# A state-space attention block and two MLPs on one core: GpSimd work in 256-column pieces, attention four levels a tile, the second MLP's weight decoding over three tiles

## The chip, the cores and the metric

The kernel runs on 1 core of one Trainium2 chip. The metric is the device time of a run in microseconds (us); three runs of the kernel before gave 609.05 to 609.72 us, with a median of 609.28 us.

## The reference

```python
def _attn_ref(x, a, B, C):                      # x (4, 8, 768, 32), B and C (4, 8, 768, 16)
    log_a = np.log(np.clip(a, 1e-06, 1.0))
    for c in range(S // 32):
        cum = np.cumsum(la, axis=-1)
        M = einsum('bhin,bhjn->bhij', Cc, Bc) * exp(cum_i - cum_j) * causal
        y[:, :, sl] = einsum('bhij,bhjd->bhid', M, xc) + einsum('bhin,bhnd->bhid', Cc, state) * exp(cum)
        state = exp(sum(la)) * state + sum_j Bc_j xc_j exp(cum_last - cum_j)

def _moe_ref(x, w_in, w_out):                   # x (3072, 256), w_in (256, 2048), w_out (2048, 256)
    h = np.maximum(x @ w_in, 0.0)
    return h * h @ w_out

def _moe2_ref(x, w_in, w_out):
    h = x @ w_in
    return (h * clip(h + 3.0, 0.0, 6.0) / 6.0) @ w_out

reference = _moe2_ref(_moe_ref(attention output as (3072, 256)))
```

## The kernel before

**Attention** runs in 12 levels of 64 positions of all four batches (NLEV). A level l is a handful of named jobs: `load` (six DMAs on SP's queue: C and B transposed, B and x by token, and last the decay factors `ef`), `scale` (GpSimd multiplies `ef` into the tile `bc`), `head` (ScalarE makes `cb` from `bc`), `tok` (GpSimd), `state` and `chunk` (TensorE bursts: the old state's part and the state's update; the part inside the level, and the next level's scores), `mask` and `adv` (VectorE), `high` and `low` (ScalarE and VectorE write the level's output as a high and a low fp32r part). Two levels make one tile of 512 tokens for the MLPs. The table PLAN says in which step of which tile each job is written.

**The first MLP** takes 6 tiles (t) of 512 tokens in 16 steps (f) of 128 hidden units; step number g = 16 t + f runs from 0 to 95. In a step (`step`, `gate`) TensorE makes h with six matmuls (`mm1`, L498), ScalarE takes the relu (L507), VectorE multiplies (L509), ScalarE makes the high part gh (L511), VectorE the low part gl (L513), and two steps later (LAG) TensorE adds h's part to y with six matmuls (`mm2`, L527). Each product is three fp32r matmuls: high by high, high by low, low by high. Levels 2 and 3 are done beside tile 0, levels 4 to 11 beside tiles 1 to 3, three levels a tile (five steps a level). After the last one the pools of the attention are closed (LASTATT) and wpool2 takes their room.

**The second MLP** takes pairs of tiles (3 pairs) in 8 quads, 24 quads g (`Quad`, `emit`). A quad is a Strassen step: seven products of sums of weights and sums of tokens (`product`, L620), ScalarE and VectorE for the gate, and 24 matmuls into y (`second`, L665). The token operands of a pair are made once: GpSimd makes the sums t1 to t4 (`oper_sum`, L565), ScalarE the high parts (`oper_high`, L576), VectorE the low parts (`oper_low`, L580).

**Weights** arrive as 64-bit floats and are decoded on the chip (`Weights`): a DMA of 512 KB a chunk j (L410), `early` on ScalarE (L421), `join` on VectorE in three operations (sign L425, bits L430, merge L435), then for the first MLP `split` (ScalarE L462, GpSimd L463), and for the second MLP `sums` (four GpSimd operations of 128 columns, L444), `high` (ScalarE, L478) and `lower` (GpSimd, 896 columns for an even chunk and 512 for an odd one, L483). The 16 chunks of the second MLP are decoded in steps 64 to 95, eight groups q of two chunks, four steps a group: join of the even chunk at step 64 + 4q, of the odd one two steps later.

The order of all this is the order in which the Python code writes it: each engine runs its instructions in that order and waits on semaphores. `at(g, point)` puts a job of the second MLP at a step (or, with 1000 added, at one of five points of a quad).

Of the kernel before, what the change touches and what calls it, by code (L numbers as in the profile page):

```python
# [964 lines left out]
```

## Time and profile before

| | us |
|---|---|
| median of three runs | 609.28 |
| the profiled execution, its own time | 613.11 |
| its span (first to last instruction) | 611.2 |
| TensorE busy (L498, L527, L620, L665 above all) | 569.9 |
| VectorE busy | 439.3 |
| ScalarE busy | 350.6 |
| GpSimd busy | 114.0 |
| mean granted TensorE clock, of full speed | 0.967 |

In the rows below PE is TensorE, PEld its weight loads, DVE VectorE, ACT ScalarE, POOL GpSimd and SP the queue that issues the DMAs. A row of the timeline gives the start in us, the duration in us, the engine, the line, the operation and its tiles with their shapes; in brackets stands how long the engine had been idle before it and what ended that. Matmul durations overlap; their starts give the pace.

### The profile page before, as it was taken

To read this page: it belongs to the slowest core of one execution; us is meant where nothing else is said; L and a number is where in the kernel's file an instruction comes from. 1 tells how busy PE (TensorE), PEld (TensorE's weight loads), DVE (VectorE), ACT (ScalarE), POOL (GpSimd) and SP (SyncE) were. 2 spreads that over 40 slices of the span, in tenths; PEclk is the share of its full clock that TensorE was granted. 3 is DMA by queue.
4 is the path that set the end of the run, shared out by engine and by line. 5 is a ranking of instruction groups with operands and counts; after the bars stand their busy time and mean duration, and the time that the engine had idled before them with its cause. 6 is when DMAs were issued, how large, how long until landed. Compare 5 with 4: busy or idle time off the path is not lost. (4 is left out here: it accounts for less than half of the span.)

```text
span 611.2 us, 11012 instructions
## 1 busy us (share of the span) xinstructions
PE 569.9 (93%) x4451; PEld 452.6 (74%) x4451; DVE 439.3 (72%) x672; ACT 350.6 (57%) x615; POOL 114.0 (19%) x117
## 2 busy tenths in 40 slices
PE   6587999999999999998987689999799999999996
PEld 3456787777778888876866468888588888788885
DVE  6598984556555545788788787677967778867674
ACT  4365755445445444664645556667666667766663
POOL 5252430011111000444355540000400000000000
PEclk9687999999999999999998889999989999999999
DMA  7771422221223000322231000000110000200002
GB/s 202 242 234 39 130 60 62 63 58 27 60 61 114 1 3 0 104 69 80 93 91 48 1 1 0 1 1 1 29 41 0 1 1 1 69 2 0 1 1 70
DMA packets 32802, 31.46 MB, mean 51 GB/s; under 512 B 14608, under 2 KB 27376, under 8 KB 32752
## 3 DMA queue, kind: packets, MB, share of 16 engines
q1 hardware_dynamic: 31408, 30.37, 17.1%
q8 instruction: 35, 0.57, 0.4%
q10 hardware_dynamic: 1344, 0.39, 0.3%
q14 instruction: 15, 0.12, 0.1%
HBM read 27.41 MB, written 3.35 MB: 50 GB/s over the span
## 5 line engine op out<-in xcount | busy, mean ns | idle before, releaser
L509 DVE TENSOR_TENSOR ga<-ga,ha 128x512 f32<-128x512 f32 x96 | 65.7, 685 | 54.6 <-ACT ga L507 54.1
L511 ACT ACTIVATE gha<-ga 128x512 fp32r<-128x512 f32 x96 | 60.8, 633 | 69.2 <-DVE ga L509 69.2
L513 DVE TENSOR_TENSOR gla<-ga,gha 128x512 fp32r<-128x512 f32 x96 | 69.8, 727 | 33.9 <-ACT gha L511 33.8
L527 PE MATMUL ya<-gla,ah 128*128 128x512 f32 x192 | 77.4, 403 | 14.1 <-DVE gla L513 14.1
L507 ACT ACTIVATE ga<-ha 128x512 f32<-128x512 f32 x96 | 56.7, 591 | 52.1 <-PE ha L498 52.1
L498 PE MATMUL ha<-act_h,ah 128*128 128x512 f32 x192 | 77.0, 401 | 5.9 <-DVE ga L509 5.1
L527 PE MATMUL ya<-gha,ah 128*128 128x512 f32 x192 | 78.4, 408 | 0.0
L665 PE MATMUL y<-glc,bh 128*128 128x512 f32 x192 | 75.8, 395 | 1.3 <-DVE glc L651 1.3
L498 PE MATMUL ha<-act_h,al 128*128 128x512 f32 x192 | 76.4, 398 | 0.0
L527 PE MATMUL ya<-gha,al 128*128 128x512 f32 x192 | 76.1, 396 | 0.0
L498 PE MATMUL ha<-act_l,ah 128*128 128x512 f32 x192 | 76.1, 396 | 0.0
L665 PE MATMUL y<-ghc,bh 128*128 128x512 f32 x192 | 75.6, 394 | 0.0
L665 PE MATMUL y<-ghc,bl 128*128 128x512 f32 x192 | 75.5, 393 | 0.0
L651 DVE TENSOR_TENSOR glc<-c,ghc 128x512 fp32r<-128x512 f32 x96 | 68.3, 715 | 6.7 <-ACT ghc L648 6.3
L634 ACT ACTIVATE rc<-c,three 128x512 f32<-128x512 f32 x72 | 51.9, 720 | 29.4 <-DVE c L629 28.9
L642 DVE SCALAR_TENSOR_TENSOR c<-rc,c 128x512 f32<-128x512 f32 x72 | 51.8, 720 | 23.3 <-ACT rc L634 23.3
L648 ACT ACTIVATE ghc<-c 128x512 fp32r<-128x512 f32 x96 | 58.2, 629 | 3.5 <-DVE c L642 3.4
L527 PEld LDWEIGHTS ya<-gla,ah 128*128 128x128 f32 x192 | 36.7, 191 | 26.5 <-DVE gla L513 18.9
L629 DVE TENSOR_TENSOR c<-Z,u 128x512 f32<-128x512 f32 x48 | 33.1, 690 | 27.6 <-PE Z L620 27.6
L498 PEld LDWEIGHTS ha<-act_h,ah 128*128 128x128 f32 x192 | 37.2, 194 | 14.6 <-DVE ga L509 5.6
L665 PEld LDWEIGHTS y<-glc,bh 128*128 128x128 f32 x192 | 36.5, 190 | 10.2 <-DVE glc L651 2.5
L625 ACT COPY u<-X 128x512 f32<-128x512 f32 x48 | 28.1, 585 | 27.6 <-PE X L620 27.6
(213 smaller groups left out, 998.1 us busy)
## 6 DMA issues: line engine op xcount, KB each, us to landing
rawa<-in_w1i SPq DMA_DIRECT2D x8, 512.0 KB
rawa<-in_w1o SPq DMA_DIRECT2D x8, 512.0 KB
rawb<-in_w2i SPq DMA_DIRECT2D x8, 512.0 KB
rawb<-in_w2o SPq DMA_DIRECT2D x8, 512.0 KB
xb<-in_x SPq DMA_DIRECT2D x24, 128.0 KB
out_yT<-xf SPq DMA_DIRECT2D x12, 256.0 KB
ef<-scr SPq DMA_DIRECT2D x10, 256.0 KB
bc<-in_cT SPq DMA_DIRECT2D x12, 128.0 KB
```

The lines of the kernel that those rows point to most:

```text
L498: nc.tensor.matmul(out=h, lhsT=wt[fb][:, k, fo * P:fo * P + P], rhs=xt[t][:, k, :], start=i == 0, stop=i == 5)
L507: nc.scalar.activation(out=g, in_=h, func=AF.Relu)
L509: nc.vector.tensor_tensor(out=g, in0=g, in1=h, op=ALU.mult)
L511: nc.scalar.activation(out=gh, in_=g, func=AF.Copy)
L513: nc.vector.tensor_tensor(out=gl, in0=g, in1=gh.bitcast(F32), op=ALU.subtract)
L527: nc.tensor.matmul(out=ys[m], lhsT=terms[i][0][fb][:, fo, m * P:m * P + P], rhs=terms[i][1], start=f == 0 and i == 0, stop=f == NF - 1 and ...
L629: nc.vector.tensor_tensor(out=self.sb[c], in0=self.ps[bank], in1=self.sb[n], op=ALU.add)
L634: nc.scalar.activation(out=self.sb["r" + c], in_=src, func=AF.Relu, bias=three)
L642: nc.vector.scalar_tensor_tensor(out=self.sb[c], in0=self.sb["r" + c], scalar=6.0, in1=src, op0=ALU.min, op1=ALU.mult)
L648: nc.scalar.activation(out=self.gh[c], in_=self.sb[c], func=AF.Copy)
L651: nc.vector.tensor_tensor(out=self.gl[c], in0=self.sb[c], in1=self.gh[c].bitcast(F32), op=ALU.subtract)
L665: nc.tensor.matmul(out=ys[t][m], lhsT=terms[i][0][:, 7 + 2 * (1 - f) + m], rhs=terms[i][1], start=first and i == 0, stop=last and i == 2, ...
```

## The change

Five things are edited. (1) GpSimd's operations of 512 and 896 columns (`scale`, `split`, `lower`, `oper_sum`) are written as pieces of 256 columns. (2) Levels 4 to 11 take four steps each, four levels a tile, so that the attention ends with tile 2 (LASTATT 3 to 2) and wpool2 opens in tile 3. (3) The 16 chunks of the second MLP's weights are decoded from step 48 on, eight groups that begin at steps 48, 54, 60, 66, 72, 79, 86 and 91 instead of every four steps from 64; `high` and `lower` come one step later after the joins. (4) The operands of pair 0 are made over steps 80 to 95 instead of 89 to 95, those of pairs 1 and 2 over the four quads before the pair instead of mostly in the last one. (5) To make room, buffers move: the first MLP's raw chunks 3 to 9 lie in other places and chunk 12's DMA is written in step 6 instead of 4, act_l of tiles 0 to 2 becomes one tile that holds group 4's weights later, and operands take turns in PLACES.

```diff
-LASTATT = 3
+LASTATT = 2
...
 for _l in range(4, 12):
-    _s = 16 * ((_l - 4) // 3 + 1) + 5 * ((_l - 4) % 3)
-    for _k, _v in ((0, (f"mask{_l}", f"tok{_l}")), (1, (f"scale{_l + 1}",)), (2, (f"state{_l}", f"head{_l + 1}")),
-                   (3, (f"chunk{_l}", f"adv{_l}", f"load{_l + 2}")), (4, (f"high{_l}",)), (5, (f"low{_l}",))):
...
+    for _k, _v in ((0, (f"mask{_l}", f"tok{_l}", f"scale{_l + 1}")), (1, (f"head{_l + 1}",)), (2, (f"state{_l}",)),
+                   (3, (f"chunk{_l}", f"high{_l}", f"adv{_l}", f"load{_l + 2}")), (4, (f"low{_l}",))):
+        _d = PLAN.setdefault((4 * _l + _k) // 16, {})
...
-QKEEP = 4
+QKEEP = 3
...
+PLACES = ("l3", "l4", "w6", "w8", "w9", "w10", "w11", "raw", "raw", "wt", "wt", "l5")
...
-        (eng or nc.gpsimd).tensor_tensor(out=flat, in0=lev[l].pop("ef"), in1=flat, op=ALU.mult)
+        n = 4 if eng else 2
+        for b in range(0, NB, n):
+            (eng or nc.gpsimd).tensor_tensor(out=flat[:, b:b + n], in0=ef[:, b:b + n], in1=flat[:, b:b + n], op=ALU.mult)
...
-            nc.gpsimd.tensor_tensor(out=lo, in0=wt, in1=hi.bitcast(F32), op=ALU.subtract)
+            for k in range(2):
+                nc.gpsimd.tensor_tensor(out=lo[:, k], in0=wt[:, k], in1=hi[:, k].bitcast(F32), op=ALU.subtract)
...
-            d = slice(s.start - 1, s.stop - 1)
-            nc.gpsimd.tensor_tensor(out=self.lo[j // 2][:, d], in0=self.wt[j // 2][:, s],
-                                    in1=self.hi[j // 2][:, d].bitcast(F32), op=ALU.subtract)
+            for i in range(s.start, s.stop, 2):
+                k = slice(i, min(i + 2, s.stop))
+                d = slice(k.start - 1, k.stop - 1)
+                nc.gpsimd.tensor_tensor(out=self.lo[j // 2][:, d], in0=self.wt[j // 2][:, k],
+                                        in1=self.hi[j // 2][:, d].bitcast(F32), op=ALU.subtract)
...
-        pool, tag = (ps_y, "y") if 16 * t + f >= 68 and f % 4 > 1 else (ps_h, "h")
+        pool, tag = (ps_y, "y") if 16 * t + f >= 52 and f % 4 > 1 else (ps_h, "h")
...
-        nc.gpsimd.tensor_tensor(out=f[n], in0=f[i0], in1=f[i1], op=ALU.subtract)
+        for k in range(2):
+            c = slice(TOK // 2 * k, TOK // 2 * (k + 1))
+            nc.gpsimd.tensor_tensor(out=f[n][:, c], in0=f[i0][:, c], in1=f[i1][:, c], op=ALU.subtract)
...
-        for j in {0: (6, 7), 1: (8,), 2: (9,), 3: (10, 11), 4: (12,), 7: (13,), 8: (14,), 10: (15,)}.get(f, ()):
+        for j in {0: (6, 7), 1: (8,), 2: (9,), 3: (10, 11), 6: (12,), 7: (13,), 8: (14,), 10: (15,)}.get(f, ()):
...
-    for q in range(NQ):
-        base = 64 + 4 * q
-        late = 2 * (q == QNEW)
+    for q, base in enumerate((48, 54, 60, 66, 72, 79, 86, 91)):
+        late = 2 * (q == QNEW + 1)
         for dg, p, f, j in ((-1, 0, "early", 0), (0, 0, "join", 0), (0, 0, "sums", 0), (1, 0, "early", 1), (2, 0, "join", 1),
-                            (2 + late, 1, "high", 0), (2 + late, 1, "lower", 0), (3 + late, 1, "high", 1),
-                            (3 + late, 1, "lower", 1)):
+                            (3 + late, 1, "high", 0), (3 + late, 1, "lower", 0), (4 + late, 1, "high", 1),
+                            (4 + late, 1, "lower", 1)):
...
-        for n, dg, p in (("t1", -2, 4), ("t2", -1, 0), ("t3", -1, 4), ("t4", 0, 0), ("b11", 0, 0)):
-            at(1000 + g + dg, p, lambda n=n: oper_sum(key, n))
-        for i, n in enumerate(OPS):
-            for d, f in ((0, oper_high), (1, oper_low)):
-                dg, p = divmod(i + d, 5)
-                at(1000 + g + dg, p, lambda f=f, n=n: f(key, n))
...
+    operands(0, ("b", 0), ((80, 0, "s", "b11"), (81, 0, "h", "b11"), (82, 0, "l", "b11"), (83, 0, "s", "t1"), (83, 0, "h", "b21"),
+                           (84, 0, "l", "b21"), (89, 0, "s", "t2"), (90, 0, "h", "t2"), (90, 0, "s", "t3"), (91, 0, "l", "t2"),
+                           (92, 0, "h", "t3"), (92, 0, "l", "t3"), (93, 0, "h", "t1"), (93, 0, "s", "t4"), (94, 0, "l", "t1"),
+                           (94, 0, "h", "t4"), (95, 0, "l", "t4"), (1000, 0, "h", "b22"), (1000, 1, "l", "b22")))
+    for p in range(1, NPAIR):
+        operands(1000 + NQ * p, ("b", p),
+                 ((-4, 0, "s", "t1"), (-4, 1, "s", "b11"), (-4, 1, "h", "b11"), (-4, 2, "l", "b11"), (-4, 3, "s", "t2"),
+                  (-4, 4, "h", "b21"), (-3, 0, "l", "b21"), (-3, 0, "s", "t3"), (-3, 2, "h", "t2"), (-3, 3, "l", "t2"),
+                  (-3, 3, "s", "t4"), (-2, 0, "h", "t3"), (-2, 1, "l", "t3"), (-2, 3, "h", "t1"), (-2, 4, "l", "t1"),
+                  (-1, 1, "h", "t4"), (-1, 2, "l", "t4"), (-1, 3, "h", "b22"), (-1, 4, "l", "b22")))
```

VectorE's order around one group of the second MLP's weights (`lowb` rows are a join; `ga` and `gla` are the two operations of every step). Before, group 3 in tile 4:

```order
L509 TENSOR_TENSOR ga_12_3402<-ga_12_3402,ha_12_3393 128x512
L425 TENSOR_SCALAR lowb_3412<-rawb_3311 128x512
L430 TENSOR_SCALAR lowb_3412<-rawb_3311 128x512
L435 SCALAR_TENSOR_TENSOR wtb_3390<-wtb_3390,lowb_3412 128x512
L513 TENSOR_TENSOR gla_12_3401<-ga_12_3402,gha_12_3400 128x512
L509 TENSOR_TENSOR ga_13_3432<-ga_13_3432,ha_13_3423 128x512
L513 TENSOR_TENSOR gla_13_3431<-ga_13_3432,gha_13_3430 128x512
L509 TENSOR_TENSOR ga_14_3453<-ga_14_3453,ha_14_3444 128x512
L425 TENSOR_SCALAR lowb_3467<-rawb_3366 128x512
L430 TENSOR_SCALAR lowb_3467<-rawb_3366 128x512
L435 SCALAR_TENSOR_TENSOR wtb_3390<-wtb_3390,lowb_3467 128x512
```

With the change, from the odd chunk of group 1 to the even one of group 2, in tile 3:

```order
L441 SCALAR_TENSOR_TENSOR wtb_2925<-wtb_2925,lowb_2998 128x512
L526 TENSOR_TENSOR gla_8_2987<-ga_8_2988,gha_8_2986 128x512
L522 TENSOR_TENSOR ga_9_3014<-ga_9_3014,ha_9_3005 128x512
L526 TENSOR_TENSOR gla_9_3013<-ga_9_3014,gha_9_3012 128x512
L522 TENSOR_TENSOR ga_10_3041<-ga_10_3041,ha_10_3032 128x512
L526 TENSOR_TENSOR gla_10_3040<-ga_10_3041,gha_10_3039 128x512
L522 TENSOR_TENSOR ga_11_3064<-ga_11_3064,ha_11_3055 128x512
L526 TENSOR_TENSOR gla_11_3063<-ga_11_3064,gha_11_3062 128x512
L522 TENSOR_TENSOR ga_12_3086<-ga_12_3086,ha_12_3077 128x512
L431 TENSOR_SCALAR lowb_3096<-rawb_2951 128x512
```

The joins were two steps apart throughout; now three steps without a join follow each group's odd chunk, and the group's `lower` falls into them.

ScalarE's order in a level (`act_h` is a level's `high`, `cb` the `head` of the level after the next one). Before, in tile 1:

```order
L374 CAST act_h_1387<-att_1450 128x2x2x64 x2
L507 ACTIVATE ga_10_1622<-ha_10_1613 128x512
L511 ACTIVATE gha_10_1620<-ga_10_1622 128x512
L507 ACTIVATE ga_11_1647<-ha_11_1638 128x512
L511 ACTIVATE gha_11_1645<-ga_11_1647 128x512
L507 ACTIVATE ga_12_1668<-ha_12_1659 128x512
L511 ACTIVATE gha_12_1666<-ga_12_1668 128x512
L283 ACTIVATE cb_1727<-bc_1580,hm 128x256 x2
```

With the change:

```order
L380 CAST act_h_1375<-att_1454 128x2x2x64 x2
L520 ACTIVATE ga_8_1603<-ha_8_1594 128x512
L524 ACTIVATE gha_8_1601<-ga_8_1603 128x512
L520 ACTIVATE ga_9_1630<-ha_9_1621 128x512
L524 ACTIVATE gha_9_1628<-ga_9_1630 128x512
L289 ACTIVATE cb_1640<-bc_1583,hm 128x256 x2
```

`head` stood four steps after the `load` of its level (`high` one step after it); now it stands two steps after (`high` is in the load's own step).

## Rows read from the trace of the kernel before

**Rows 1.** Busy us by stretch: PE, PEld, DVE, ACT, POOL; then PEclk, DMA share, GB/s.

```profile
260.00:346.00 86.00, 73.56 (x310) 58.49 (x309) 71.27 (x94) 47.90 (x83) 42.42 (x41) 0.98 0.23 68
351.40:366.70 15.30, 13.50 (x50) 9.82 (x49) 13.22 (x15) 8.69 (x16) 6.13 (x4) 0.89 0.01 1
443.10:458.40 15.30, 15.08 (x59) 12.29 (x60) 10.24 (x17) 9.46 (x16) 0.00 (x0) 0.89 0.15 41
```

**Rows 2.** Timeline of PE: first matmul of mm1, and the same one step later.

```profile
259.41 0.39 PE L498 MATMUL ha<-act_h,ah 128*128 128x512 f32 x1
262.13 0.39 PE L498 MATMUL ha<-act_h,ah 128*128 128x512 f32 x1
```

**Rows 3.** Timeline of ACT, L533: y of tiles 3, 4 and 5 copied out.

```profile
245.32 1.27 ACT L533 COPY xf<-ya 128x512 f32<-128x512 f32 x2
293.75 1.07 ACT L533 COPY xf<-ya 128x512 f32<-128x512 f32 x2
351.24 1.06 ACT L533 COPY xf<-ya 128x512 f32<-128x512 f32 x2
```

**Rows 4.** Timeline of PE, tiles 4 and 5: matmuls that waited for gla.

```profile
265.19 0.50 PE L527 MATMUL ya<-gla,ah 128*128 128x512 f32 x1 [1.09 <-DVE gla L513]
328.90 0.80 PE L527 MATMUL ya<-gla,ah 128*128 128x512 f32 x1 [3.09 <-DVE gla L513]
344.98 0.50 PE L527 MATMUL ya<-gla,ah 128*128 128x512 f32 x1 [3.59 <-DVE gla L513]
```

**Rows 5.** Timeline of DVE, tile 4: a join beside GpSimd's work, and one alone.

```profile
261.54 2.27 DVE L430 TENSOR_SCALAR lowb<-rawb 128x512 uint16<-128x512 uint16 x1
264.45 0.68 DVE L513 TENSOR_TENSOR gla<-ga,gha 128x512 fp32r<-128x512 f32 x1
268.08 0.42 DVE L425 TENSOR_SCALAR lowb<-rawb 128x512 uint32<-128x512 uint32 x1
268.54 0.48 DVE L430 TENSOR_SCALAR lowb<-rawb 128x512 uint16<-128x512 uint16 x1
269.73 0.69 DVE L513 TENSOR_TENSOR gla<-ga,gha 128x512 fp32r<-128x512 f32 x1
```

**Rows 6.** Timeline of POOL: `lower` of 896 columns, `scale` of 512, `tok` of 256.

```profile
261.36 2.13 POOL L483 TENSOR_TENSOR bl<-wtb,bh 128x896 fp32r<-128x896 f32 x1 [1.53 <-ACT bh L478]
105.80 1.30 POOL L274 TENSOR_TENSOR bc<-ef,bc 128x512 f32<-128x512 f32 x1 [17.59 <-DMA ef<-scr]
107.05 0.63 POOL L289 TENSOR_TENSOR xb<-xb,ft 128x256 f32<-128x256 f32 x1
```

**Rows 7.** Groups by line: `bits` of the second MLP; busy us, mean ns, idle before.

```profile
L430 DVE TENSOR_SCALAR lowb<-rawb 128x512 uint16<-128x512 uint16 x16 | 22.0, 1373 | 0.6
```

**Rows 8.** Timelines of POOL and DVE, first quad.

```profile
352.65 1.60 POOL L565 TENSOR_TENSOR fb1t<-xf,fb1t 128x512 f32<-128x512 f32 x1
353.04 1.75 DVE L580 TENSOR_TENSOR olb0t<-fb0t,ohb0t 128x512 fp32r<-128x512 f32 x1
```

**Rows 9.** Timeline of PE: the first quad.

```profile
350.85 0.50 PE L620 MATMUL X<-ob0t,bh 128*128 128x512 f32 x1 [0.56 <-ACT u L625]
354.85 0.51 PE L620 MATMUL X<-olb0t,bh 128*128 128x512 f32 x1 [1.28 <-DVE olb0t L580]
```

**Rows 10.** Timeline of PE: first quad of pair 1.

```profile
439.22 0.50 PE L665 MATMUL y<-glc,bh 128*128 128x512 f32 x1 [0.98 <-DVE glc L651]
443.32 0.50 PE L620 MATMUL Z<-ohb1b,bh 128*128 128x512 f32 x1 [2.21 <-DVE c L629]
```

**Rows 11.** Timelines of SP, DVE, ACT, PE: a level in tile 1.

```profile
101.85 0.61 SPq L261 DMA_DIRECT2D ef<-scr  x1
104.05 0.69 DVE L513 TENSOR_TENSOR gla<-ga,gha 128x512 fp32r<-128x512 f32 x1 [0.70 <-ACT gha L511]
106.10 0.63 ACT L511 ACTIVATE gha<-ga 128x512 fp32r<-128x512 f32 x1 [0.76 <-DVE ga L509]
107.66 0.39 PE L527 MATMUL ya<-gla,ah 128*128 128x512 f32 x1
```

More of the change, by code (lines that the diff above doesn't have):

```diff
@@ L95, in act @@
         d = act_h if k == "h" else act_l
+        if k == "l" and not d:
+            low = actp.tile([P, 3, 2, TOK], F32R, tag="l012", name="act_l012")
+            d.update({i: low[:, i] for i in range(3)})
         if t not in d:
@@ L404, in dma @@
         def dma(self, j):
-            if self.pre == "a" and 2 <= j < 11:
-                t, k = (1, "h") if j == 2 else (2 + (j - 3) // 2, "hl"[(j - 3) % 2])
+            if self.pre == "a" and 2 <= j < 10:
+                t, k = ((1, "h"), (2, "h"), (3, "h"), (3, "l"), (4, "h"), (4, "l"), (5, "h"), (5, "l"))[j - 2]
                 raw = actp.tile([P, 2, 256, 2], U32, tag=f"{k}{t}", name=f"rawa{j}")
@@ L470, in slots @@
             if q not in self.hi:
-                pl, i = (wpool2[0], f"b{q}") if q < QNEW else (wpool1, q - QNEW)
-                self.hi[q] = pl.tile([P, 11, P], F32R, tag=f"wh{i}", name=f"bh{q}")
-                self.lo[q] = pl.tile([P, 11, P], F32R, tag=f"wl{i}", name=f"bl{q}")
+                if q == QNEW:
+                    t = actp.tile([P, 24, P], F32R, tag="l012", name=f"bhl{q}")
+                    self.hi[q], self.lo[q] = t[:, 0:11], t[:, 11:22]
+                else:
+                    pl, i = (wpool2[0], f"b{q}") if q < QNEW else (wpool1, q - QNEW - 1)
+                    self.hi[q] = pl.tile([P, 11, P], F32R, tag=f"wh{i}", name=f"bh{q}")
+                    self.lo[q] = pl.tile([P, 11, P], F32R, tag=f"wl{i}", name=f"bl{q}")
             return slice(8, 12) if j % 2 else slice(1, 8)
@@ L564, in oper_sum @@
         f[n] = buffer("t" + n[1], F32, f"f{key[0]}{key[1]}{n}")
-        nc.gpsimd.tensor_tensor(out=f[n], in0=f[i0], in1=f[i1], op=ALU.subtract)
+        for k in range(2):
+            c = slice(TOK // 2 * k, TOK // 2 * (k + 1))
+            nc.gpsimd.tensor_tensor(out=f[n][:, c], in0=f[i0][:, c], in1=f[i1][:, c], op=ALU.subtract)
     def oper_high(key, n):
         d = oper[key]
-        i = OPS.index(n)
-        if i < 5:
-            t = actp.tile([P, 2, TOK], F32R, tag=f"l{i}", name=f"o{key[0]}{key[1]}{n}")
+        h = PLACES[(7 * key[1] + OPS.index(n)) % len(PLACES)]
+        name = f"o{key[0]}{key[1]}{n}"
+        if h[0] == "w" and h != "wt":
+            for k in "hl":
+                d[k][n] = wpool1.tile([P, TOK], F32R, tag=f"w{k}{h[1:]}", name=f"{name}{k}")
+        elif h == "wt":
+            t = stagep.tile([P, 12, P], F32R, tag="wt", name=name, bufs=2).rearrange("p s n -> p (s n)")
+            d["h"][n], d["l"][n] = t[:, 0:TOK], t[:, TOK:2 * TOK]
+        else:
+            t = stagep.tile([P, 2, TOK], F32R, tag="raw", name=name, bufs=2) if h == "raw" else actp.tile(
+                [P, 2, TOK], F32R, tag=h, name=name)
             d["h"][n], d["l"][n] = t[:, 0], t[:, 1]
-        else:
-            for k in "hl":
-                d[k][n] = buffer(f"o{i}{k}", F32R, f"o{k}{key[0]}{key[1]}{n}")
         nc.scalar.activation(out=d["h"][n], in_=d["f"][n], func=AF.Copy)
@@ L886, in attn_mlp_mlp, with operands @@
     for j in range(2):
[L887 to L907 removed]
+        at(45 + j, 0, lambda j=j: w2.dma(j))
+    def operands(g, key, plan):
+        for dg, p, f, n in plan:
+            at(g + dg, p, lambda f={"s": oper_sum, "h": oper_high, "l": oper_low}[f], n=n: f(key, n))
+    operands(0, ("b", 0), ((80, 0, "s", "b11"), (81, 0, "h", "b11"), (82, 0, "l", "b11"), (83, 0, "s", "t1"), (83, 0, "h", "b21"),
[3 rows of a table added]
+    for p in range(1, NPAIR):
+        operands(1000 + NQ * p, ("b", p),
[4 rows of a table added]
     def ready_second(t, f):
@@ L913, in attn_mlp_mlp @@
         for f in range(NF):
-            if (t, f) == (LASTATT + 1, 0):
+            if (t, f) == (LASTATT + 1, 1):
                 attn_ctx.close()
```

24 lines of the change are left out of this document (5 added, 19 removed).

## The prediction

> **What bounds the kernel now.** I read the busy time by stretch first, then what TensorE waited for, then VectorE's and GpSimd's timelines at those places. The list of TensorE's waits has none in tiles 1 to 3, so there only its own work counts. In tiles 4 and 5 it is busy for 73.56 of 86.00 us, while VectorE is busy for 71.27 and GpSimd for 42.42 [rows 1]; before and after, GpSimd is nearly idle. TensorE's pace without waits is 2.72 us a step: the same matmul of mm1 comes back 2.72 us later, after twelve matmuls [rows 2], so one matmul is 0.227 us and a tile of 16 steps 43.5 us. Tile 4 took 293.75 - 245.32 = 48.4 us and tile 5 took 57.5 us [rows 3].
>
> Every wait in these tiles is mm2's third matmul waiting for VectorE's gla [rows 4]. The first, 1.09 us at 265.19, is explained by the rows just ahead of it: VectorE's `bits` took 2.27 us, where the same operation takes 0.48 us two steps later [rows 5]. It ran beside GpSimd's `lower` of 896 columns, 261.36 to 263.49 [rows 6], and ended 0.3 us after that. So 1.79 us went to waiting, and gla ended at 265.13, 0.06 us ahead of the matmul that needed it. Over all 16 chunks `bits` took 22.0 us instead of 16 x 0.48 = 7.7 [rows 7]: 14.3 us of VectorE's time. At the end of tile 5, where joins, operand parts and GpSimd's sums share the same steps, the waits grow to 3.09 and 3.59 us [rows 4].
>
> **The change part by part.**
>
> *Decoding over 48 steps.* VectorE's work per step is ga and gla, at most 0.69 us each, 1.38; a join takes 269.73 - 268.08 = 1.65 us [rows 5]. Over 32 steps that was 44.2 + 26.4 for 16 joins + 14.3 of waiting + six operand parts of 0.69 (4.1) = 89 us, against 87.0 of TensorE (32 x 2.72): over the limit. Over 48 steps it is 66.2 + 26.4 + 4.1 = 96.7 us against 130.6: 74%. As important, `lower` now falls into steps without a join, as the orders show, so `bits` should take about 0.5 us each. Without its 1.79 us the wait of 1.09 is gone with 0.7 us to spare. What tile 4 can give back is 48.4 - 43.5 = 4.9 us. Tile 5's stretch to the copy at 351.24 also holds the first nine matmuls of quad 0 (2.0 us), so its floor is 45.6 and it can give back 11.9; of this two waits of about 0.55 each for ScalarE's copies in the first quad, one of them at 350.85 [rows 9], come from the quad's own chain and stay: 10.8 us.
>
> *Into the quads.* The wait of 1.28 us for an operand's low part at 354.85 [rows 9] goes, since six of the seven operands are now complete before the quads begin and the last, b22, enters the quad's last product. The granted clock in the stretch 351.4 to 366.7 was 0.89 [rows 1], after the waits of rows 4 and 9: some 3.4 us at 1.2 instead of 2.4 GHz, 0.11 x 15.3 = 1.7 us lost. With no wait of that size ahead, I take this back too. Slow matmuls inside tiles 4 and 5 are already in the tile times.
>
> *Operands over four quads.* In the first quad of pair 1 TensorE waited 0.98 and 2.21 us [rows 10], while seven low parts and the four sums of the next pair crowded VectorE; the clock was 0.89 in the stretch behind [rows 1], 1.7 us again. Spread over three to four quads a quad gets two low parts (1.4 us): 3.2 + 1.7 = 4.9 us go. A smaller wait in pair 2 I leave out of the sum.
>
> *GpSimd in pieces.* A piece of 256 columns takes 0.63 us (`tok`), one of 512 columns 1.30 [rows 6], so two pieces cost nothing extra, and GpSimd has room for more. A blocked VectorE operation then waits for the rest of one piece, at most 0.63 instead of up to 2.13. I count nothing for this by itself: it keeps the waits that remain below the slack. Cover gone, the price is rival B.
>
> *Attention in four steps a level.* The same operations, TensorE full before and after: 0. What is moved is the distance from `load` to `head`, four steps to two, on ScalarE. In the level of [rows 11] `ef`, the sixth DMA of its load on SP's queue, is issued at 101.85 and GpSimd's `scale` starts with its landing at 105.80 [rows 6], 3.95 us later; it ends at 107.10. ScalarE's gha two steps after the load ends at 106.73 [rows 11], and there `head` now stands: 0.4 us of waiting, or none, since `low` and `mask` now share a step ahead of it and push gha back. Queued behind `head` is the next relu; that chain has slack: gla starts at 104.05, ends at 104.74 and is used at 107.66, 2.9 us later [rows 11]. Taken: 0. Ends: 0 and 6 heads x 0.4 = 2.4 us. VectorE adds 3 to 4 us a level to 4 x 1.38, in some 13 us.
>
> *Tile 0.* Chunk 12's DMA now waits for join 10 (step 6), with `load4` behind it on SP's queue; ScalarE reads the chunk in step 7. The nearest row for a landing is 3.95 us (`ef`, half the bytes) against a step of at least 2.72: between 0 and 1.2 us, or 2 with the larger chunk. I take 0, since steps are longer than 2.72 where VectorE decodes in all of them. `load4` is needed in step 9. A gain of up to 1 from the pieces is as possible.
>
> *Left over.* Steps 89 to 95 still hold two joins, four operand parts, `lower` of four chunks and three sums: VectorE 7 x 1.38 + 2 x 1.65 + 4 x 0.69 = 15.7 of 19.0 us, plus waits for pieces. Between 0 and rival A's 5.4; near the low end, since the load is 83% here and was over 100% before: I take 1.0 us back.
>
> **Sum:** 4.9 + 10.8 + 1.3 + 1.7 + 4.9 - 1.0 = 22.6 us. The profiled execution took 613.1 us (span 611.2 and 1.9 around it), 3.8 above the median; from the median 609.3 the forecast is **586.7 us**.
>
> **Rivals.**
>
> *A. The end of tile 5 stays crowded.* Half of what tile 5 should give back stays lost, 5.4 us in place of the 1.0 above: 591.1 us. For it: three sums, four `lower` and four operand parts within seven steps, and ScalarE's `high` of an operand waits for GpSimd's sum. Against: the joins there fall from three to two and `bits` is rarely beside a `lower`.
>
> *B. VectorE waits as long as before, in smaller portions.* A GpSimd operation and a VectorE operation with two SBUF inputs take turns: the sum at 352.65 ran 1.60 us, VectorE's 0.69 us operation issued at 353.04 took 1.75 and ended after it [rows 8]. Pieces let VectorE in sooner, but behind it the next piece goes first, so all of GpSimd's 42 us could still be charged to VectorE. If each of the eight groups keeps its 1.09 us wait (8.7) and the end of tile 5 is as in A (5.4), in place of the 1.0: 586.7 + 13.1 = 599.8 us. Against it: with 26% of VectorE's time free and 0.7 us to spare, a portion of 0.63 fits into the slack. The Trainium skill's page "SBUF — State Buffer" (Who interferes with whom) has this rule: whichever of the two comes first holds the shared port pair for its whole instruction and the other blocks fully. By that rule splitting shortens a wait but saves no port time; the turns in the trace agree.
>
> *C. Slower: `head` holds up ScalarE.* If `ef` lands d us later than the 3.95 in the trace, each of the six heads of levels 6 to 11 holds ScalarE for 0.4 + d, and TensorE waits for what exceeds 2.9. To eat 22.6 us a head must cost 3.8, so d must pass 6.3 us; at d = 7 the time is 586.7 + 6 x 4.5 = 613.7 us. For it: six DMAs in a row on one queue, and `head` in an in-order queue that feeds every gate. Against: the other levels before show about the same distance, and a level's bytes are only spread over four steps instead of five.
>
> *D. Nothing moves:* a buffer in its new place (the joint tile of act_l, wh7, "raw") comes free so late that the decoding still bunches at the end: 609 us. I found no such reader.
>
> **How the numbers follow.** Forecast 0.74, A 0.13, B 0.07, C 0.03, D 0.03. The forecast's own range is 582 to 590: all 23.6 us plus pair 2's wait and a gain in tile 0 on one side, 2.4 for heads and 1 to 2 for tile 0 on the other. With A (589 to 595) the range is 582 to 595; B, C and D, 13 in 100, and tails are left out. A measurement of this kernel tells some 0.2% (1.2 us) from no change. Faster: forecast, A and B, 0.94; same: D, 0.03; slower: C, 0.03.
>
> **What would show it.** TensorE busy without a wait from 92 us to the quads; tiles 3 to 5 at 43.5 to 46 us each; `bits` near 0.5 us throughout; granted clock 1.00 from 92 us on; no operand row among the waits of the quads; `scale` still some 4 us after `ef` is issued. I am wrong if gla still holds TensorE in tiles 3 to 5 (B), if waits above 1 us stand at the end of tile 5 (A), or if relu waits behind cb in tiles 1 and 2 (C).

## The result, and the profile after

The changed kernel took **588.5 us** (median of 6 runs, 586.6 to 589.8) beside 609.2 us for the kernel before (6 runs, 608.5 to 610.6): a ratio of 0.9655, 95% interval 0.9633 to 0.9677. The forecast was 586.7 us, range 582 to 595. The profiled execution took 587.0 us, span 585.3.

From the page of the changed kernel (share of the span and instructions of each engine; the granted clock in 40 slices):

```profile
PE 560.7 (96%) x4451; PEld 448.9 (77%) x4451; DVE 423.6 (72%) x672; ACT 354.4 (61%) x615; POOL 137.9 (24%) x187
...
PEclk9797999999999999999999999999999999999999
```

Behind the first 60 us the granted clock no longer falls (1.00 from 60 to 585 us). The copies that end tiles 3, 4 and 5, which answer to [rows 3]:

```profile
242.47 1.27 ACT L546 COPY xf<-ya 128x512 f32<-128x512 f32 x2
...
285.99 1.27 ACT L546 COPY xf<-ya 128x512 f32<-128x512 f32 x2
...
333.59 1.05 ACT L546 COPY xf<-ya 128x512 f32<-128x512 f32 x2
```

Tile 4 takes 43.52 us, 16 x 2.72, where it took 48.4. Tile 5 takes 47.60, where it took 57.5. These are the distances between ScalarE's copies; between TensorE's own last products of tiles 4 and 5 lie 45.88 us, before 56.63 (349.89 less 293.26):

```profile
286.25 0.39 PE L540 MATMUL ya<-gla,ah 128*128 128x512 f32 x1
...
332.13 0.39 PE L540 MATMUL ya<-gla,ah 128*128 128x512 f32 x1
```

```profile
293.26 0.39 PE L527 MATMUL ya<-gla,ah 128*128 128x512 f32 x1
...
349.89 0.40 PE L527 MATMUL ya<-gla,ah 128*128 128x512 f32 x1
```

By stretch (columns as in [rows 1]; tile 4, tile 5, first quads, first quads of pair 1):

```profile
242.50:286.00 43.50, 43.50 (x193) 36.05 (x192) 30.21 (x47) 26.56 (x45) 17.22 (x26) 1.00 0.21 61
286.00:333.60 47.60, 45.59 (x197) 36.33 (x196) 36.91 (x54) 30.44 (x53) 27.65 (x37) 1.00 0.11 34
333.60:349.00 15.40, 14.25 (x61) 10.98 (x60) 12.49 (x18) 10.94 (x19) 5.53 (x7) 1.00 0.00 1
418.30:434.30 16.00, 15.30 (x67) 12.34 (x67) 12.17 (x20) 10.71 (x18) 0.00 (x0) 1.00 0.18 50
```

The 0.89 of both quad stretches in [rows 1] is 1.00. In tile 4 TensorE is busy all the time and VectorE for 30.21 us. All that TensorE waits for after 290 us (total, times, longest):

```profile
PE ya L540 <- DVE gla L526: 1.5, 2, 0.8
PE Z L638 <- DVE c L647: 1.4, 2, 0.7
PE X L638 <- ACT u L643: 1.2, 1, 1.2
PE X L638 <- ACT s L643: 0.6, 1, 0.6
```

No operand is among them, as [rows 9] had one. Three of them lie in tile 5:

```profile
319.13 0.50 PE L540 MATMUL ya<-gla,ah 128*128 128x512 f32 x1 [0.76 <-DVE gla L526]
...
322.84 0.50 PE L540 MATMUL ya<-gla,ah 128*128 128x512 f32 x1 [0.69 <-DVE gla L526]
...
330.19 0.50 PE L638 MATMUL X<-ob0t2h,bh 128*128 128x512 f32 x1 [0.56 <-ACT s L643]
```

A join of tile 4 on VectorE, which answers to [rows 5], and GpSimd around it:

```profile
262.13 0.42 DVE L431 TENSOR_SCALAR lowb<-rawb 128x512 uint32<-128x512 uint32 x1
262.58 0.48 DVE L436 TENSOR_SCALAR lowb<-rawb 128x512 uint16<-128x512 uint16 x1
263.16 0.69 DVE L441 SCALAR_TENSOR_TENSOR wtb<-wtb,lowb 128x512 uint32<-128x512 uint32 x1
263.77 0.69 DVE L526 TENSOR_TENSOR gla<-ga,gha 128x512 fp32r<-128x512 f32 x1
...
254.95 4.15 POOL L496 TENSOR_TENSOR bl<-wtb,bh 128x256 fp32r<-128x256 f32 x5
```

`lower` ends 3 us ahead of this join, so `bits` has no neighbour. As groups (busy, mean ns of one; [rows 7] for `bits` before):

```profile
L436 DVE TENSOR_SCALAR lowb<-rawb 128x512 uint16<-128x512 uint16 x16 | 7.9, 496 | 0.5
...
L496 POOL TENSOR_TENSOR bl<-wtb,bh 128x256 fp32r<-128x256 f32 x35 | 31.5, 924 | 33.6 <-ACT bh L489 33.6
...
L289 ACT ACTIVATE cb<-bc,hm 128x256 f32<-128x256 f32 x24 | 10.9, 500 | 4.5 <-POOL bc L280 2.2 <-DVE bc L280 1.9
```

`bits` fell from 22.0 to 7.9 us. A piece of `lower` with 256 columns takes 0.92 us on average, not the 0.63 I took from `tok`. ScalarE's `head` waited 2.2 us in all for GpSimd's `scale`, in three heads (the rest of the 4.5 is one wait for VectorE).

Cutting also has a price of its own. `split` does the same work whole in the kernel before, in pieces of 256 columns with the change, and in pieces of 128 in run 10 (shortest, median and longest in ns):

```profile
L463 POOL TENSOR_TENSOR al<-wta,ah x16: 1277/1295/1643, 13.3 to 83.9; 128x512 fp32r<-128x512 f32 x16
...
L470 POOL TENSOR_TENSOR al<-wta,ah x32: 726/745/1178, 13.3 to 81.8; 128x256 fp32r<-128x256 f32 x32
...
L466 POOL TENSOR_TENSOR al<-wta,ah x64: 452/468/910, 13.2 to 87.7; 128x128 fp32r<-128x128 f32 x64
```

By the medians two pieces of 256 take 1.49 us and four of 128 take 1.87, where one of 512 takes 1.30: some 0.19 us more for each cut.

### The profile page after: what moved, and what is told of

Same layout as the page of the kernel before. It is cut to its first block, busy times and chain, and to the rows that moved or that the text cites. A ratio compares the mean times of both kernels' runs of the same rounds, so it can differ in the third digit from the quotient of the medians.

```text
span 585.3 us, 11093 instructions
## 1 busy us (share of the span) xinstructions
PE 560.7 (96%) x4451; PEld 448.9 (77%) x4451; DVE 423.6 (72%) x672; ACT 354.4 (61%) x615; POOL 137.9 (24%) x187
## 4 chain that ended last, share of the span: by engine, by line
PE 83%; DVE 7%; issue 3%; ACT 2%; DMA 2%; SPq 1%; POOL 1%; DVEq 0%; ACTq 0%; POOLq 0%
PE y L683 21%; PE ya L540 20%; PE ha L511 19%; PE X L638 10%; PE Z L638 5%; PE V L638 2%; PE att L326 1%; PE att L340 1%; PE att L306 1%; DMA rawa<-in_w1i 1%; DVE gla L526 1%; DVE ga L522 1%; PE att L354 1%; SPq L257 1%; DVE c L660 1%
## 5 line engine op out<-in xcount | busy, mean ns | idle before, releaser
L526 DVE TENSOR_TENSOR gla<-ga,gha 128x512 fp32r<-128x512 f32 x96 | 75.6, 787 | 32.7 <-ACT gha L524 32.4
L540 PE MATMUL ya<-gla,ah 128*128 128x512 f32 x192 | 76.1, 396 | 3.0 <-DVE gla L526 3.0
L683 PE MATMUL y<-glc,bh 128*128 128x512 f32 x168 | 65.7, 391 | 0.1
L683 PE MATMUL y<-ghc,bh 128*128 128x512 f32 x168 | 65.5, 390 | 0.0
L683 PE MATMUL y<-ghc,bl 128*128 128x512 f32 x168 | 65.4, 390 | 0.0
L540 PEld LDWEIGHTS ya<-gha,ah 128*128 128x128 f32 x192 | 36.4, 190 | 9.4 <-issue 1.9
L511 PEld LDWEIGHTS ha<-act_l,ah 128*128 128x128 f32 x192 | 36.7, 191 | 8.1 <-DVE act_l L385 0.3
```

The costliest lines, as they stand in the source:

```text
L511: nc.tensor.matmul(out=h, lhsT=wt[fb][:, k, fo * P:fo * P + P], rhs=xt[t][:, k, :], start=i == 0, stop=i == 5)
L526: nc.vector.tensor_tensor(out=gl, in0=g, in1=gh.bitcast(F32), op=ALU.subtract)
L540: nc.tensor.matmul(out=ys[m], lhsT=terms[i][0][fb][:, fo, m * P:m * P + P], rhs=terms[i][1], start=f == 0 and i == 0, stop=f == NF - 1 and ...
L683: nc.tensor.matmul(out=ys[t][m], lhsT=terms[i][0][:, 7 + 2 * (1 - f) + m], rhs=terms[i][1], start=first and i == 0, stop=last and i == 2, ...
```

## The experiments

Twelve kernels ran, on several chips; each has runs of the kernel before beside it, so ratios compare. The traces say more, because everything after tile 0 repeats to about 0.1 us (one exception below). The stages, in us, are read at ScalarE's copies that end a tile and at VectorE's copy of a pair's second output; "rest" is the span after the end of tile 0. A copy can come later than TensorE's last product, so small shifts between tile 5 and pair 0 can be the mark's.

| kernel | median | before | ratio, 95% interval | end of tile 0 | tile 4 | tile 5 | pair 0 | pair 1 | rest |
|---|---|---|---|---|---|---|---|---|---|
| before | 609.2 | | | 91.43 | 48.43 | 57.49 | 90.74 | 84.63 | 519.8 |
| before again | 610.0 (one) | 611.2 | | 89.50 | 48.43 | 57.48 | 89.64 | 84.66 | 518.6 |
| changed | 588.5 | 609.2 | 0.966, 0.963 to 0.968 | 88.58 | 43.52 | 47.60 | 84.74 | 82.60 | 496.7 |
| changed again | 588.7 | 611.0 | 0.963, 0.960 to 0.966 | 91.83 | 43.52 | 47.57 | 84.76 | 82.61 | 496.8 |
| 1 pieces alone | 601.2 | 609.5 | 0.986, 0.982 to 0.989 | 88.60 | 46.60 | 54.95 | 86.31 | 83.00 | 509.3 |
| 2 pieces undone | 591.4 | 609.5 | 0.971, 0.967 to 0.975 | 88.45 | 43.52 | 50.60 | 84.48 | 82.60 | 499.5 |
| 3 decoding in 32 steps | 598.4 | 609.5 | 0.981, 0.977 to 0.985 | 87.78 | 46.61 | 54.69 | 84.41 | 82.61 | 506.6 |
| 4 operands crowded | 588.2 | 609.5 | 0.965, 0.962 to 0.969 | 89.56 | 43.52 | 47.57 | 85.81 | 83.02 | 498.1 |
| 5 first operands crowded | 589.3 | 611.2 | 0.965, 0.961 to 0.968 | 88.44 | 43.52 | 47.78 | 85.24 | 82.60 | 497.5 |
| 6 whole and crowded | 596.2 | 611.2 | 0.975, 0.972 to 0.978 | 90.70 | 43.52 | 50.61 | 87.05 | 84.63 | 504.1 |
| 7 whole and 32 steps | 605.0 | 611.2 | 0.990, 0.987 to 0.993 | 90.94 | 48.43 | 57.74 | 84.55 | 82.64 | 511.7 |
| 8 end of tile 5 | 588.6 | 611.0 | 0.963, 0.959 to 0.966 | 90.16 | 43.52 | 47.80 | 84.40 | 82.59 | 496.5 |
| 9 end and sums later | 585.6 | 611.0 | 0.958, 0.955 to 0.960 | 88.96 | 43.52 | 47.01 | 83.59 | 82.60 | 494.9 |
| 10 pieces of 128 | 602.4 | 611.0 | 0.984, 0.981 to 0.988 | 92.79 | 44.35 | 57.71 | 85.00 | 83.03 | 508.4 |

Tiles 1 to 3 together take 153.8 to 154.0 us in all of them, attention in four steps a level or in five; pair 2 takes 79.5 in all.

**1. Pieces alone.** The four GpSimd edits of the change in the kernel before; of `lower`:

```diff
-            d = slice(s.start - 1, s.stop - 1)
-            nc.gpsimd.tensor_tensor(out=self.lo[j // 2][:, d], in0=self.wt[j // 2][:, s],
+            for i in range(s.start, s.stop, 2):
+                k = slice(i, min(i + 2, s.stop))
...
```

> The kernel before, with GpSimd's operations in pieces of 256 columns and nothing else changed. My theory: with the decoding still in 32 steps VectorE stays at its limit there, so the pieces alone bring 0 to 4 us, 605 to 609 us, and the bits rows fall from 22.0 us to no less than about 14, since each of the pieces still holds VectorE up once. Rival (the pieces were the main part): 601 us or less, with tile 4 down from 48.4 to about 44 us. Second rival (pieces cost GpSimd time and the gain of 2.85 us up to the end of tile 0 does not come from them): the copy that ends tile 0 stays at 91.4 us.

Measured: 8.4 us faster by the runs (601.2 against 609.5), at the edge of what the rival said; by the traces after tile 0 it is 9.3 to 10.5. Tile 4 fell to 46.60, less far than the rival's 44. My 0 to 4 us was wrong, and so were my 14 us for `bits`, which fell from 22.0 to 10.9: tiles 4 and 5 gave 4.4 us, and pairs 0 and 1, which I had not thought of, 5.0 (against the second trace of the kernel before). VectorE, then GpSimd, at a join of tile 4 that has pieces beside it:

```profile
257.77 0.42 DVE L427 TENSOR_SCALAR lowb<-rawb 128x512 uint32<-128x512 uint32 x1
258.23 0.90 DVE L432 TENSOR_SCALAR lowb<-rawb 128x512 uint16<-128x512 uint16 x1
259.16 1.07 DVE L437 SCALAR_TENSOR_TENSOR wtb<-wtb,lowb 128x512 uint32<-128x512 uint32 x1
260.15 1.23 DVE L518 TENSOR_TENSOR gla<-ga,gha 128x512 fp32r<-128x512 f32 x1
...
258.05 5.05 POOL L488 TENSOR_TENSOR bl<-wtb,bh 128x256 fp32r<-128x256 f32 x6 [1.52 <-ACT bh L481]
```

Where `bits` had been held up once, for 1.79 us, three VectorE operations now each lose 0.4 to 0.55 us (0.90, 1.07 and 1.23, where the join shown above has 0.48, 0.69 and 0.69), and GpSimd waits as well: its six pieces take 5.05 us, where their medians without VectorE beside them would give some 4.2 (an estimate from `split`).

**2. Pieces undone.** The same edits taken back in the changed kernel.

> The changed kernel with GpSimd's operations whole again; decoding, attention and operands as changed. My theory: 0 to 4 us slower than the changed kernel (588.5 to 592.5), tile 4 still at 43.5 us, since lower falls into steps without a join; what comes back comes at the end of tile 5 and in tile 0 (its end back from 88.6 to about 91.4 us if the pieces brought that gain). Rival (the pieces were the main part): 597 us or more and tile 4 above 46 us.

Measured: 591.4 against 588.5, 2.9 us, all of it in tile 5 (50.60 against 47.60). Under the slower decoding, tile 4 does not need the pieces, and the end of tile 5 does: TensorE's longest wait for gla there grows from 0.76 to 1.76 us, and the granted clock of the stretch falls from 1.00 to 0.97. Tile 0 does not move.

**3. Decoding in 32 steps.**

```diff
-    for q, base in enumerate((48, 54, 60, 66, 72, 79, 86, 91)):
-        late = 2 * (q == QNEW + 1)
+    for q in range(NQ):
+        base = 64 + 4 * q
+        late = -1
...
-        at(45 + j, 0, lambda j=j: w2.dma(j))
+        at(61 + j, 0, lambda j=j: w2.dma(j))
```

> The changed kernel with the second MLP's weights decoded in 32 steps again, four steps a pair of chunks from tile 4 on, with lower two and three steps behind the first join, as before the change; pieces, attention and operands stay as changed. My theory: the sum's terms for tiles 4 and 5 come back, 4.9 and about 9.9 us, less what the pieces hide: 599 to 604 us, tile 4 at 46 to 48.4 us. Rival (with pieces VectorE gets in soon enough, so that the pace of the decoding no longer counts): 588 to 592 us, tile 4 at 43.5 to 44 us.

Measured: 598.4, between the two and 0.6 below my range. Tile 4 costs 3.1 us more and tile 5 7.1; both match the kernel with pieces alone to 0.3 us, so these two edits, pieces and pace, settle what tiles 4 and 5 take.

**4. Operands crowded.** The highs and lows of pairs 1 and 2 at the points where they stood before:

```diff
-                 ((-4, 0, "s", "t1"), (-4, 1, "s", "b11"), (-4, 1, "h", "b11"), (-4, 2, "l", "b11"), (-4, 3, "s", "t2"),
...
+                 ((-3, 4, "s", "t1"), (-2, 0, "s", "t2"), (-2, 4, "s", "t3"), (-1, 0, "s", "t4"), (-1, 0, "s", "b11")) + tuple(
+                     (-1 + (i + d) // 5, (i + d) % 5, "hl"[d], n) for i, n in enumerate(OPS) for d in range(2)))
```

> The changed kernel with the operands of pairs 1 and 2 put into the last quad of the pair ahead and the first two points of the next, as before the change; their new buffers and the pieces stay. My theory: the term of 4.9 us comes back, 3.2 of waits at the first quad of pair 1 and about 1.7 of the clock behind them: 592 to 594 us, with a wait above 1 us for VectorE's c near the first quad of pair 1 and a granted clock below 0.95 in the stretch behind. Rival (the waits came from GpSimd's whole sums, which are in pieces now): 588 to 589.5 us.

Measured: 588.2, no loss that the runs can tell, where I expected 4 to 5 us; the time is the rival's. The trace has 1.07 us in pair 0 and 0.42 in pair 1. The wait for c, 0.70 us in the changed kernel, is back at 1.66; the clock stays at 1.00. TensorE's wait, and the stretch from 419.5 us on:

```profile
421.70 0.50 PE L638 MATMUL Z<-ob1b,bh 128*128 128x512 f32 x1 [1.66 <-DVE c L647]
...
419.50:435.50 16.00, 14.34 (x64) 11.55 (x63) 12.41 (x20) 9.91 (x17) 2.21 (x3) 1.00 0.18 51
```

**5. First operands crowded.** Pair 0's operands back at steps 89 to 95 and in the first points of quad 0.

> The changed kernel with the operands of pair 0 made as before, from step 89 into the third point of quad 0; all else as changed. My theory after the first four experiments: with pieces the waits for operands stay short whatever their place, 588.5 to 590.5 us, what is lost being at the end of tile 5. Rival (the prediction's term for the way into the quads): the wait of 1.28 us for an operand's low part and 1.7 us of clock come back, and the end of tile 5 is fuller: 591.5 us or more, granted clock below 0.95 in the stretch behind tile 5.

Measured: 0.5 us in pair 0 and 0.2 in tile 5 by the trace, nothing by the runs. No operand's low part is waited for; TensorE waits once for 2.7 us, for ScalarE's s in the first quad, and in return no longer for gla at the end of tile 5. The granted clock behind tile 5 is 0.97. So beside pieces 0.7 us comes back of the 3.0 that the prediction had for the way into the quads; without pieces this was not run.

**6. Whole and crowded.** The edits of 2 and 4 together.

> The changed kernel with whole GpSimd operations and the operands of pairs 1 and 2 in one quad, the two edits that cost 2.9 and about 0 us by themselves. My theory: spreading the operands and cutting GpSimd's sums in pieces are two cures of the same wait, so either alone hides it and only undoing both brings the 4.9 us back: 594 to 597 us, with a wait of about 2 us for VectorE's c at the first quad of pair 1 and a granted clock near 0.9 behind it. Rival (the two have nothing to do with each other, and the wait went for another reason, such as the new buffers): 591 to 592.5 us.

Measured: 596.2, and by the stages exactly the lost term: against the run with whole operations alone, pair 0 takes 2.57 us more and pair 1 2.03, 4.6 in all. The same wait, and the 16 us behind it:

```profile
427.08 0.50 PE L631 MATMUL Z<-ob1b,bh 128*128 128x512 f32 x1 [2.22 <-DVE c L640]
...
427.00:443.00 16.00, 15.92 (x63) 13.00 (x64) 10.66 (x18) 10.38 (x18) 0.00 (x0) 0.89 0.13 36
```

So the full wait of 2.21 us [rows 10] and the clock of 0.89 behind it [rows 1], a part of the stretch at 1.2 instead of 2.4 GHz, come back only when both cures are taken away; crowding alone had brought the wait back to 1.66 us (run 4). The clock agrees in five traces: behind a wait of 2.2 us it was 0.89 in both executions of the kernel before and here, behind one of 1.65 or 1.66 us it was 1.00 in runs 1 and 4.

**7. Whole and 32 steps.** The edits of 2 and 3 together.

> The changed kernel with whole GpSimd operations and the decoding in 32 steps, the two edits that cost 2.9 and 9.9 us by themselves; attention and operands stay as changed. My theory: pieces and the slower pace of decoding cure the same waits too, so that together they cost more than the sum, near what pieces brought to the kernel before (8.4) on top of 598.4: 604 to 608 us, tile 4 near 48.4 and tile 5 near 57 us. Rival (they add): 600.5 to 602.5 us.

Measured: 605.0. Tiles 4 and 5 take 106.17 us, as before the change (105.92). The four combinations of these tiles:

| tiles 4 and 5, us | whole operations | pieces of 256 |
|---|---|---|
| decoding in 32 steps | 106.17 | 101.30 |
| decoding in 48 steps | 94.12 | 91.12 |

Pieces bring 4.9 us at the old pace and 3.0 at the new one; the pace brings 12.1 with whole operations and 10.2 with pieces. They overlap by 1.9 us, in the direction that I expected.

**The two kernels again.**

> The kernel before once more, unchanged, for a second trace of it. My theory: up to the end of tile 0 an execution varies by itself, since that end lay at 87.8 to 89.6 us in five kernels with the same or nearly the same tile 0; the second trace then ends tile 0 anywhere from 88 to 91.5 us and has the same times as the first from there on (tile 4 48.4, tile 5 57.5, quads 260.0 us, each within 0.5). Rival (the 2.85 us that tile 0 ends earlier in the changed kernel come from the change): the second trace ends tile 0 at 91.4 us again, within 0.3.

> The changed kernel once more, unchanged, on the chip of the two runs ahead of it. Theory: from the end of tile 0 to the end of the span 496.7 us again, within 0.3, whatever the start takes. Rival (what follows tile 0 varies from run to run as well): off by more than 0.6 us.

After tile 0 both kernels repeat, but for one stage: in the second trace of the kernel before the first quads had a granted clock of 1.00, not the 0.89 of [rows 1], and pair 0 took 1.10 us less, so that the quads did not repeat within the 0.5 us that I had expected. The time at 1.2 GHz lay earlier there, at the end of tile 5, in part while TensorE waited anyway:

```profile
344.00:347.40 3.40, 3.22 (x8) 2.08 (x7) 2.83 (x3) 2.03 (x5) 1.33 (x2) 0.50 0.00 0
349.40:364.70 15.30, 13.27 (x55) 9.72 (x54) 13.67 (x16) 9.42 (x16) 6.20 (x4) 1.00 0.00 1
```

The end of tile 0 moves from run to run, 87.8 to 92.8 us over all kernels. In the changed kernel's two executions, VectorE's wait for a weight chunk and TensorE's wait behind it:

```profile
25.33 0.43 DVE L431 TENSOR_SCALAR lowa<-rawa 128x512 uint32<-128x512 uint32 x1 [2.04 <-DMA rawa<-in_w1o]
...
28.54 0.80 PE L511 MATMUL ha<-act_h,ah 128*128 128x512 f32 x1 [2.55 <-DVE ga L522]
```

```profile
29.62 0.43 DVE L431 TENSOR_SCALAR lowa<-rawa 128x512 uint32<-128x512 uint32 x1 [6.32 <-DMA rawa<-in_w1o]
...
32.83 0.79 PE L511 MATMUL ha<-act_h,ah 128*128 128x512 f32 x1 [8.65 <-DVE ga L522]
```

**8 and 9. A faster version.** By the prediction's floor of 45.6 us tile 5 still lost 2.0 (that floor is too high, see the next section). I moved the last two decode groups forward and re-ordered pair 0's operands, and in a second kernel also held back the next pair's sums by a copy of one column on GpSimd that reads the running pair's third quad (GATE is 2):

```diff
-    for q, base in enumerate((48, 54, 60, 66, 72, 79, 86, 91)):
+    for q, base in enumerate((48, 54, 60, 66, 72, 79, 85, 89)):
...
+        if cur and g % NQ == GATE and g < NQ * (NPAIR - 1):
+            nc.gpsimd.tensor_copy(out=gates, in_=cur.sb["s1"][:, 0:1])
```

> The changed kernel with the last two decode groups moved one and two steps forward (85 and 89 for 86 and 91) and pair 0's operands re-ordered so that no high part is asked for in the step after its GpSimd sum's turn and none is left for quad 0. My theory: what tile 5 still loses above its floor (47.6 against 45.6 us) is ScalarE waiting for a sum behind lower and gla waiting behind two decode groups; 1 to 2 us go, tile 5 at 45.6 to 46.6 us. Rival (the same work merely crowds earlier steps): tile 5 at 47.4 us or more. The three sums of the next pair still follow at once on GpSimd, so pair 0 stays at 84.5 to 85 us.

> The run of this call with the end of tile 5 relieved, and besides one copy of 128x1 on GpSimd ahead of each next pair's four sums, which reads a result of the running pair's third quad, so that these sums no longer run beside the first quads. My theory: VectorE's operations of 1.15 to 1.23 us in the first quads are back at 0.68 and the wait of 1.15 us for ScalarE's u goes with them: pair 0 at 83 to 84 us instead of 84.7, 2 to 3.5 us in all against the changed kernel. Rival (u is late because of the two copies at the end of tile 5, whatever GpSimd does): pair 0 stays at 84.5 us or more.

The first alone brings nothing: tile 5 stays at 47.80, its two waits for gla turned into one of 1.3 us. With the sums later tile 5 is 47.01 and pair 0 83.59, 1.8 us less after tile 0 than the changed kernel. Between TensorE's last products tile 5 takes 45.84 us in both, as in the changed kernel (45.88): the gain lies in the first quads, and tile 5's shorter time is its copy alone. The runs give 585.6 against 588.7 us for the changed kernel on the same chip (3.0 us, more than the traces show; the intervals against the kernel before, 0.955 to 0.960 and 0.960 to 0.966, just touch). VectorE's operation in the first quads is back at 0.69 us from 1.15, and the wait for u shrinks from 1.15 to 0.70:

```profile
332.11 0.69 DVE L662 SCALAR_TENSOR_TENSOR c<-rc,c 128x512 f32<-128x512 f32 x1 [0.79 <-ACT rc L654]
...
334.96 0.50 PE L640 MATMUL X<-ob0t4h,bh 128*128 128x512 f32 x1 [0.70 <-ACT u L645]
...
349.61 0.19 POOL L719 COPY gates<-s 128x1 f32<-128x1 f32 x1 [22.16 <-ACT s L645]
```

**10. Pieces of 128 columns**, in the kernel before.

> The kernel before with GpSimd's operations in pieces of 128 columns instead of 256, nothing else changed. My theory (what counts is the longest single portion a VectorE operation waits, not the sum of the portions): tile 4 falls below the 46.6 us of pieces of 256, to 45 to 46.3, and the time to 597 to 600 us. Rival (VectorE gives up about the same time in all, and its load sets the end): tile 4 within 0.3 of 46.6 us, 600 to 602.5 us.

Measured: half of each. Tile 4 falls to 44.35, further than I expected, but tile 5 is back at 57.71, and the whole is no better than with 256. Tiles 4 and 5 before, with pieces of 256, and with pieces of 128:

```profile
245.30:293.75 48.45, 45.19 (x197) 36.37 (x197) 39.67 (x56) 29.00 (x51) 21.99 (x24) 1.00 0.29 86
293.75:351.20 57.45, 47.22 (x191) 36.72 (x190) 47.10 (x60) 32.13 (x57) 29.16 (x28) 0.94 0.19 55
```

```profile
242.50:289.00 46.50, 45.09 (x196) 36.37 (x195) 38.85 (x56) 28.90 (x50) 28.43 (x40) 1.00 0.30 90
289.00:344.00 55.00, 46.92 (x190) 36.04 (x189) 44.67 (x60) 32.33 (x57) 38.02 (x49) 0.95 0.19 58
```

```profile
246.60:291.00 44.40, 44.40 (x197) 36.62 (x196) 36.30 (x55) 29.31 (x51) 33.85 (x60) 1.00 0.31 95
291.00:348.70 57.70, 48.42 (x191) 36.17 (x190) 40.79 (x61) 32.17 (x58) 46.59 (x81) 0.91 0.19 55
```

VectorE's time (third figure after the length) falls from 39.67 to 38.85 and 36.30 in tile 4 and from 47.10 to 44.67 and 40.79 in tile 5; GpSimd's (the fifth) rises from 21.99 to 28.43 and 33.85, and from 29.16 to 38.02 and 46.59. Smaller pieces hand the waiting from VectorE to GpSimd and add the price of each cut. With 128 columns GpSimd is busy for 81% of tile 5, its sums come late, and ScalarE's operand highs wait for them:

```profile
333.75 0.63 ACT L584 ACTIVATE ob0t<-fb0t 128x512 fp32r<-128x512 f32 x1 [3.18 <-POOL fb0t L573]
...
342.42 0.63 ACT L584 ACTIVATE ob0t<-fb0t 128x512 fp32r<-128x512 f32 x1 [2.02 <-POOL fb0t L573]
```

## Why the prediction was right, and which step failed

The sum was 22.6 us. After tile 0 the changed kernel is 23.1 us shorter than the first trace of the kernel before and 21.9 shorter than the second; the medians differ by 20.6, the ratio of the runs allows 19.7 to 22.4. The start, whose end moved by 3.3 us between two executions of the changed kernel, blurs the medians.

- **Decoding over 48 steps.** Tile 4: 4.9 forecast, 4.91 measured. Tile 5: 10.8 less 1.0 forecast, 9.89 measured. That this agrees is in part luck, since the floor of 45.6 us was wrong: it adds the first nine matmuls of quad 0, but does not take off the twelve of tile 5's first two steps, which TensorE does before tile 4's last product. From one last product to the other are 189 matmuls, 42.9 us at 0.227. TensorE took 56.63 before and 45.88 with the change, so it got back 10.8 and still loses 3.0, of which the three waits of 0.76, 0.69 and 0.56 us are 2.0. Tile 5 missed its 43.5 to 46 us. `bits` fell to 0.50 us each. But 3.0 of the 9.9 us are the pieces' (run 2), which I had costed at nothing.
- **Into the quads, and operands over four quads.** 3.0 and 4.9 forecast; pairs 0 and 1 together gave 8.0 us against the first trace and 7.0 against the second. The 1.7 us for the clock in the first quads was read from one execution; in the second the clock fell earlier. Beside pieces only 0.7 of the 3.0 us hangs on where pair 0's operands stand (run 5). Of pair 1's waits, 0.70 us for c stays. GpSimd was not nearly idle behind tile 5, as I wrote, but busy for 6.13 of 15.30 us [rows 1], with the next pair's sums; run 9 moved them away.
- **GpSimd in pieces: the step that failed.** "I count nothing for this by itself": by themselves pieces gave 8.4 us. They cure the same waits as the other two parts. Added last, to the slower decoding and the spread operands, they give 2.9 us (run 2); and the spread operands, which I credited with 4.9 us, give 4.6 without pieces and 1.5 with them (runs 6 and 4). The total came out because each wait was counted once, not because its cure was named rightly.
- **A piece's duration.** That two pieces cost nothing extra was wrong: 0.63 us holds for `tok`, but a piece of `split` of the same size takes 0.745 by the median, so that two cost 0.19 us more than one whole, and a piece of `lower` takes 0.92 on average. GpSimd had the room (137.9 us of 585).
- **Attention in four steps.** 0 forecast; tiles 1 to 3 took 153.9 us before and after. `head` waited 2.2 us in all, within my 0 to 2.4, though in three heads and up to 1.35 in one. `scale` started 3.9 to 4.6 us after `ef` was issued, and TensorE had no wait in tiles 1 to 3, so rival C had no ground.
- **Tile 0.** 0 forecast. The 2.85 us between the two profiled executions are run-to-run: with the change it ended between 87.8 and 91.8 us, without it at 88.6 to 92.8.
- **Rival A** held in part: gla is still waited for twice at the end of tile 5, though never for 1 us, and TensorE loses 3.0 us there, where A amounts to 6.5 and the forecast to 2.1, each with the 1.1 of the quad's own chain. **Rival B** was right about the mechanism: beside pieces, VectorE's time fell by only 3.2 of 86.8 us in tiles 4 and 5 (runs with 32 steps). It was wrong that TensorE would pay the same: with pieces alone TensorE's waits shrank and these tiles gave 4.4 us. My reading, which no run isolates: portions of 0.4 to 0.55 us fit in part into VectorE's slack, as the wait of 1.79 did not. VectorE and GpSimd together were busy for 137.9 us in tiles 4 and 5 before, 150.0 with pieces of 256 and 157.5 with pieces of 128; a part of the rise is the price of the cuts. The rule of the Trainium skill's page "SBUF — State Buffer" (Who interferes with whom), that whichever comes first has the shared port pair for its whole instruction while the other blocks, is in line with this: splitting shortened the wait and saved no time in the sum.

Left open: what would free tile 5 of its last waits, since moving decode groups left TensorE's 45.8 us as they were; and the order of attention by itself, which no run undid.

## What to carry to other kernels

When several parts of a change cure the same wait, count the wait once and test each part with and without the others: here operands crowded cost 1.5 us beside pieces and 4.6 beside whole operations. Cutting one engine's long operations shortens the longest wait it imposes, not the sum, and pays where the remaining portion fits the slack; it costs the cut engine time, here 0.19 us a cut and its own waits, so stop before that engine is late itself. Compare traces by stage from the first point that repeats: after tile 0 two executions of the changed kernel agreed within 0.1 us, while their whole times differed by 3.3. Count a floor between two marks by the work that lies between them, and look whether the mark itself moved.

## What the runs showed of the hardware that I had not expected

- GpSimd's `lower` in the kernel before takes 28.6 us in 16 whole operations; the same columns take 41.8 us in pieces of 256 and 53.3 in pieces of 128 (group totals). By the medians of `split` the pieces alone would take some 33 and 41 us (estimates); the rest is time lost beside VectorE.
- A TensorE wait of 1.66 us ahead of the quads of pair 1 left the granted clock at 1.00 (run 4); one of 2.22 us, after two shorter waits of 0.30 and 0.99, was followed by 16 us at 0.89 (run 6). The same program had 0.89 in the first quads of one execution and 1.00 in those of another, where the fall lay at the end of tile 5.
- The landing of one early weight chunk differs by 4.3 us between two executions of one kernel (VectorE idle for 2.04 or 6.32 us), and tile 0 ended 3.3 us later in the second. It is not the only cause: in run 7 that operation started at 26.23 us, near the earlier of the two, and tile 0 ended at 90.94.
